# The second head's GpSimd operations in an attention and mixture-of-experts kernel, over all 128 partitions

## The chip, the cores and the metric

One core of a Trainium2 chip runs the whole kernel. The metric is the device time of one execution in microseconds (us). The kernel before takes 857.82 us, the median of three runs from 856.32 to 862.12 us. The rows below come from one profiled execution of it.

## The reference

The first part is causal attention over 8 batches of 8 heads, 576 tokens and 64 features each. To the scaled scores a bias from a running sum is added, and what lies behind the diagonal is masked. The second part sends every one of the 4608 rows of 512 to one of eight experts, the one with the largest gate logit.

```python
s_pos = np.maximum(s, 0.0)
cum = np.cumsum(s_pos, axis=-1)
bias = -(cum[:, :, :, None] - cum[:, :, None, :])
scores = np.where(causal, -1000000000.0, scores + np.minimum(bias, 0.0))
attn = np.exp(scores - np.max(scores, axis=-1, keepdims=True))   # then divided by its sum, times v
...
expert_idx = np.argmax(x @ w_gate, axis=1)
out[mask] = gate_w[mask, None] * (np.maximum(xe @ w1[e], 0.0) @ w2[e])
```

## The kernel before, in words

**Pairs.** Attention works on 32 pairs of heads, one pair after the other. Head 0 of a pair lies on partitions 0 to 63 and head 1 on 64 to 127. The 576 queries are cut into five groups. Groups 0 to 3 hold 128 queries of one head each. The last 64 queries of both heads make one *mixed* group (`MIX`): its q is laid out block-diagonally in a tile `qd`, head 0 in one quarter and head 1 in the other, with zeros elsewhere. There are two `qd` tiles, used in turn.

**Precision by halves.** q and k are each split into a high part and a low part (`q`, `kh`, `kl`). The scores of a group are three products: high by `kh`, high by `kl`, low by `kh`. In each pair TensorE (PE) begins with group 0, and its second product needs `kl`.

**The engines in a pair.** ScalarE (ACT) makes `kh`, the exponentials and some copies out of PSUM. VectorE (DVE) makes `z` (scores plus the mask table `B`, with the row's extreme) and other copies, among them `xb`, the attention output of a pair, once per pair. GpSimd (POOL) makes the high part of q (`QH`, line 198), `kl` (`KL`, line 210), the causal entries of the mask table (`DM`, lines 149 and 162 to 172), the low part of q (`QL`, line 203) and `qd` (`QD`, line 214), in this order. Before the change, `qd` is two copies, one for each head's 64 partitions, and the causal entries of the mixed group are two selects, again one for each head.

**Routing.** Four pairs are one batch. While the next four pairs run, the batch before is routed. Its 576 rows go to DRAM with five indirect DMAs per batch (*scatters*, line 465), which POOL issues: at `SD`, between the low part of q and `qd`, in two pairs of four, and at `SC`, between `kl` and the mask table, in three of four (the names are those of the table `ORDER`; all five are `xs<-xr,dsi` in the trace). The rows come from a tile `xr` with two buffers, so that a batch writes into the buffer that was used two batches earlier. `fresh` (line 351, an iota on POOL) is the first to write into it.

**Order.** The order of each engine's work inside the pair loop is written out by hand: `ORDER` lists one step per token, and all engines except SyncE (SP) keep that order. The framework adds a semaphore wait to an instruction wherever it sees a dependence. Waits on `DMASW` are for DMAs that POOL has issued, `DMAHW` for those of SP and ACT.

**After attention** the eight experts run one after the other, almost all of it matmuls on PE.

Of the kernel before, what the change touches and what calls it, by code (L numbers as in the profile page):

```python
# [8 lines left out]
F32 = mybir.dt.float32  # L9
# [4 lines left out]
AF = mybir.ActivationFunctionType  # L14
ALU = mybir.AluOpType
# [4 lines left out]
P, HP = 128, 64  # L20
# [33 lines left out]
UB, UW = 768, 1536  # L54
# [18 lines left out]
class Attention:  # L73
    def __init__(self, ctx, tc, K, qkv, s, rt, ps_t):
        self.tc, self.nc, self.K, self.qkv, self.rt, self.ps_t = tc, tc.nc, K, qkv, rt, ps_t
        nc = tc.nc
        pool = lambda name, bufs: ctx.enter_context(tc.tile_pool(name=name, bufs=bufs))
        self.open, self.st, self.nfill = True, {}, 0
        self.ldx, c0, self.lq, self.ld, self.ldv = (
            pool("a_x", 4), pool("a_c0", 1), pool("a_q", 2), pool("a_k", 2), pool("a_v", 4),  # L80
        )
        self.wk, c1, cp, self.sm = pool("a_wk", 4), pool("a_c1", 1), pool("a_c", 1), pool("a_sm", 10)
        self.qd = [c0.tile([P, 2, 2, HP], F32R, name=f"qd{i}") for i in range(2)]
        self.Es = [c1.tile([P, 2, w], F32, name=f"E{g}") for g, w in enumerate(TW[:4])]
        self.Es.append(c1.tile([P, 640], F32, name="E4"))
        self.aT = [(c0, cp)[i].tile([P, 5, 2, S], F32, name=f"aT{i}") for i in range(2)]
        self.ps_s = ctx.enter_context(tc.tile_pool(name="ps_s", bufs=2, space=PSUM))
        self.tab = pool("a_tab", 4)
        flat = self.aT[1].rearrange("p a h c -> p (a h c)")
        raw, cum, zz = (flat[:, S * x : S * x + S] for x in range(3))  # L90
        nc.vector.memset(zz, 0.0)
        for h in range(2):
            nc.sync.dma_start(raw[64 * h : 64 * h + 64], s)
        self.load(0)
        for i in range(2):
            nc.scalar.activation(
                self.qd[i].rearrange("p a h c -> p (a h c)"), zz[:, : 4 * HP], AF.Copy
            )
        self.eye = cp.tile([P, 3, HP], BF16, name="eye")
        self.tri = cp.tile([P, P], BF16, name="tri")  # L100
        low = self.Es[0][:, 0]
        nc.gpsimd.memset(low, 0.0)
        for h in range(2):
            self.keep_causal(low[64 * h : 64 * h + 64], low[64 * h : 64 * h + 64], [[-1, P]])
        nc.vector.tensor_scalar(out=raw, in0=raw, scalar1=0.0, scalar2=8.0, op0=ALU.max, op1=ALU.mult)
        nc.vector.tensor_tensor_scan(
            out=cum, data0=raw, data1=zz, initial=0.0, op0=ALU.add, op1=ALU.add
        )
        tc.keep_in_program_order(nc.scalar.dma_start(K["cum"], cum[:64]))
        self.load(1)  # L110
        self.load_v(0)
        self.cum = cum
        self.sel = cp.tile([P, 3, P], F32, name="sel")
        for x, h, c in (0, 0, slice(0, P)), (1, 65, slice(0, P)), (2, 0, slice(0, HP)), (2, 1, slice(HP, P)):
            one = K["ident"][:, h : h + 1]
            nc.vector.tensor_copy(self.sel[:, x, c], one.broadcast_to([P, c.stop - c.start]))
        b = self.st[0]["B"] = self.tab.tile([P, UW + S], F32, name="B")
        nc.gpsimd.memset(b, 0.0)
        for p in 1, 2:
            self.table(p)  # L120
        for part in (0, 2, 1, 3, 4):
            self.split(0, part)
        nc.vector.memset(self.eye, 0.0)
        nc.vector.tensor_tensor(
            out=self.eye[:, 1], in0=K["ident"][:, :HP], in1=K["ident"][:, HP:], op=ALU.add
        )
        nc.vector.tensor_copy(self.tri, low)

        warm = self.ps_s.tile([P, 2, 512], F32, name="s")[:, 0]
        zb = zz.bitcast(BF16)  # L130
        for _ in range(WARM):
            nc.tensor.matmul(warm, zb[:, :P], zb[:, P : P + 512], start=True, stop=True)
        for g in ORD[:2]:
            self.first_bias(g)
        nc.gpsimd.memset(self.Es[MIX][:, S:], 0.0)
        self.LT = rt.tile([P, 640], F32, name="LT", bufs=1)
        nc.gpsimd.memset(self.LT[:, S:], 0.0)
        self.xb, self.sums, self.sumx, self.rr, self.ra = [], [], [], [], []
        for i in range(2):
            self.xb.append(rt.tile([P, 4, 640], F32, name=f"xb{i}", bufs=1))  # L140
            nc.gpsimd.memset(self.xb[i][:, :, S:], 0.0)
            self.sums.append(rt.tile([P, 4, 8], F32, name=f"sums{i}", bufs=1))
            self.sumx.append(rt.tile([P, 4], F32, name=f"sumx{i}", bufs=1))
            self.rr.append(rt.tile([P, 5, 8], F32, name=f"rr{i}", bufs=1))
            nc.gpsimd.memset(self.rr[i][:, 4], 1.0)
            self.ra.append(rt.tile([P, 2, 5, 4], F32, name=f"ra{i}", bufs=1))
# [18 lines left out]
    def causal(self, p):  # L165
        t = self.st[p]["B"]
        b = t[:, :UW].rearrange("p (h k c) -> p h k c", h=2, c=P)
        self.keep_causal(b[:, :, 4:], b[:, :, :2], [[0, 2], [0, 2], [-1, P]])
        self.keep_causal(b[:, :, 3], b[:, :, 3], [[0, 2], [-1, P]])
        for h in range(2):  # L170
            x = t[64 * h : 64 * h + 64, UW + 512 :]
            self.keep_causal(x, x, [[-1, 64]])

    def load(self, p):
        x = self.ldx.tile([P, 2 * S], F32, name="qk")
# [15 lines left out]
    def split(self, p, part):  # L191
        nc = self.nc
        d = self.st[p]
        q, k = d["x"][:, :S], d["x"][:, S:]
        if part == 0:
            d["q"] = self.lq.tile([P, 2, S], F32R, name="q")
            if p > 1:
                nc.gpsimd.tensor_copy(d["q"][:, 0], q)
            else:
                nc.scalar.activation(d["q"][:, 0], q, AF.Copy)  # L200
        elif part == 1:
            e = nc.gpsimd if p > 1 else nc.vector
            e.tensor_tensor(out=d["q"][:, 1], in0=q, in1=d["q"][:, 0].bitcast(F32), op=ALU.subtract)
        elif part == 2:
            d["kh"] = self.ld.tile([P, S], F32R, name="kh")
            nc.scalar.activation(d["kh"], k, AF.Copy)
        elif part == 3:
            d["kl"] = self.ld.tile([P, S], F32R, name="kl")
            e = nc.gpsimd if p > 1 else nc.vector
            e.tensor_tensor(out=d["kl"], in0=k, in1=d["kh"].bitcast(F32), op=ALU.subtract)  # L210
        else:
            for h in range(2):
                r = slice(64 * h, 64 * h + 64)
                nc.gpsimd.tensor_copy(self.qd[p % 2][r, :, h], d["q"][r, :, 512:].bitcast(F32))

    def mms(self, groups, diagonal=None, begin=True):
        for n in range(len(groups[0][1])):
# [798 lines left out]
```

## Time and profile before

| | us |
|---|---|
| median of three runs | 857.82 |
| the profiled execution | 858.59 |
| its span, first to last instruction | 856.9 |
| PE busy in the span | 779.1 (91%) |
| DVE busy | 465.7 (54%) |
| ACT busy | 420.0 (49%) |
| POOL busy | 257.2 (30%) |
| mean granted clock of PE, as a share of full speed | 0.954 |

The 1.7 us between span and time are start and end of the execution. PE's clock has two levels here, 2.4 GHz (1.00) and 1.2 GHz (0.50), and a mean between them is a share of time at each. The pair loop fills about the first 393 us of the span, the experts the rest. `xb` copies mark the pairs on DVE, and some of them serve as borders of stretches below: they start at 71.97, 100.20, 138.07, 188.37, 237.57, 286.30 and 335.99 us, with three pairs in the first and in the second of these stretches and four in each later one.

### The profile page before, as it was taken

The page shows a single profiled execution, that of the slowest core. Times are in us where ns is not written, and L with a number is a line of the kernel's source. Part 1 is how long each engine was busy: PE and PEld are TensorE (multiplying, and loading weights), DVE is VectorE, ACT ScalarE, POOL GpSimd, SP SyncE. Part 2 cuts the span into 40 slices and gives each one's busy share as a digit, 9 for nine tenths or more (in the row PEclk, how much of TensorE's full clock was granted, in tenths as well). Part 3 has the DMA queues.
Part 4 walks back from the last instruction along what each step waited for, and adds up shares of the span by engine and source line. Part 5 has one row for each costly group of instructions (what it writes and reads, how often), then busy time and mean ns, then how long its engine had stood idle before and what let it go on. Part 6 is the DMA issues. An engine that isn't in the chain of part 4 may idle for free.

```text
span 856.9 us, 17576 instructions
## 1 busy us (share of the span) xinstructions
PE 779.1 (91%) x6664; PEld 603.3 (70%) x6664; DVE 465.7 (54%) x1234; ACT 420.0 (49%) x1003; POOL 257.2 (30%) x393
## 2 busy tenths in 40 slices
PE   7899979869796887888989999999999999999995
PEld 4667647656565666665778878788888888888874
DVE  4778858666685866766533536263264254442611
ACT  3788867757685676665313425151252242432510
POOL 4565556465455546632210010101001000001001
PEclk8999999988898998989999999999999999999998
DMA  7899745545554465144892626162062053440100
GB/s 246 241 285 305 201 140 183 186 146 155 185 188 134 162 194 157 54 161 149 265 280 79 212 74 222 64 222 87 26 205 105 26 176 125 158 165 28 54 28 37
DMA packets 57345, 130.80 MB, mean 153 GB/s; under 512 B 5456, under 2 KB 5456, under 8 KB 57233
## 3 DMA queue, kind: packets, MB, share of 16 engines
q1 hardware_dynamic: 48768, 105.53, 38.7%
q0 software_dynamic: 5936, 18.92, 5.9%
q10 hardware_dynamic: 2528, 4.89, 1.8%
q8 instruction: 67, 1.10, 0.5%
q14 instruction: 46, 0.37, 0.1%
HBM read 101.30 MB, written 28.27 MB: 151 GB/s over the span
## 4 chain that ended last, share of the span: by engine, by line
issue 36%; PE 11%; DMA 6%; another core or an unknown queue 3%; POOL 3%; DVE 2%; ACT 1%; POOLq 1%; DVEq 0%
DMA out_dram<-y,xr 6%; PE ph L723 3%; PE py L745 3%; POOL out_dram L752 2%; PE s L227 2%; PE t L336 2%; PE t L303 1%; DVE z L285 0%; DVE xr L456 0%; ACT aT L326 0%; PE s L303 0%; ACT E L299 0%; POOLq L845 0%; PE t L695 0%
## 5 line engine op out<-in xcount | busy, mean ns | idle before, releaser
L299 ACT ACTIVATE E<-z,m 128x128 f32<-128x128 f32 (+4 forms) x288 | 166.2, 581 | 96.8 <-DVE m L285 92.5
L745 PE MATMUL py<-w2t,hT 128*128 128x512 f32 x768 | 181.3, 392 | 1.0 <-DVEq L859 1.0
L723 PE MATMUL ph<-xT,w1t 128*128 128x512 f32 x768 | 177.7, 391 | 1.7 <-ACT xT L627 1.2
L723 PEld LDWEIGHTS ph<-xT,w1t 128*128 128x128 f32 x768 | 143.3, 188 | 33.0 <-issue 2.1
L745 PEld LDWEIGHTS py<-w2t,hT 128*128 128x128 f32 x768 | 142.6, 188 | 31.3 <-issue 1.4
L752 POOL DMA_INDIRECT out_dram<-y,xr x39 | 37.7, 966 | 397.4 <-DVE y L751 332.2
L285 DVE CUSTOM_DVE_ANT_0 z<-s,B 128x128 f32<-128x128 f32 (+3 forms) x224 | 114.0, 542 | 61.8 <-PE s L227 41.2
L227 PE MATMUL s<-kh,q 64*128 64x256 f32 (+3 forms) x512 | 102.9, 401 | 5.3 <-DVE m L285 4.0
L336 PE MATMUL t<-aT,v 128*64 128x64 f32 (+4 forms) x1152 | 97.4, 325 | 1.4 <-issue 0.7
L303 PE MATMUL t<-ident,E 64*128 64x64 f32 x1600 | 85.3, 237 | 5.5 <-issue 1.5
L751 DVE TENSOR_SCALAR y<-py,xr 128x512 f32<-128x512 f32 x35 | 26.3, 751 | 114.5 <-PE py L745 114.5
L725 ACT ACTIVATE hT<-ph 128x512 fp32r<-128x512 f32 x64 | 38.3, 598 | 102.2 <-PE ph L723 95.0
L303 PEld LDWEIGHTS t<-ident,E 64*128 64x128 f32 x1600 | 72.2, 148 | 17.9 <-issue 6.1
L227 PE MATMUL s<-kl,q 64*128 64x128 f32 (+3 forms) x256 | 46.6, 351 | 38.1 <-POOL kl L210 38.0
L726 DVE SCALAR_TENSOR_TENSOR hT<-ph,hT 128x512 fp32r<-128x512 f32 x64 | 44.1, 691 | 68.2 <-ACT hT L725 64.6
L227 PEld LDWEIGHTS s<-kh,q 64*128 64x128 f32 x512 | 55.6, 205 | 35.1 <-DVE m L285 14.6
L326 ACT COPY aT<-t 128x768 f32<-128x768 f32 (+2 forms) x96 | 73.2, 794 | 12.6 <-PE t L303 9.9
L336 PEld LDWEIGHTS t<-aT,v 128*64 128x64 f32 x1152 | 52.0, 142 | 23.5 <-issue 13.3
L149 POOL TENSOR_SCALAR_AFFINE_SELECT B<-B 64x64 f32<-64x64 f32 (+2 forms) x128 | 46.4, 385 | 50.3 <-issue 45.8
L227 PEld LDWEIGHTS s<-kl,q 64*128 64x128 f32 x256 | 27.8, 205 | 41.1 <-POOL kl L210 40.5
L299 ACT ACTIVATION_READ_ACCUMULATOR E<-z,m 128x1 f32 x288 | 54.9, 191 | 0.0
L465 POOL DMA_INDIRECT xs<-xr,dsi x40 | 40.1, 1002 | 34.3 <-issue 18.6
(156 smaller groups left out, 986.9 us busy)
## 6 DMA issues: line engine op xcount, KB each, us to landing
raw<-in_w_dram SPq DMA_DIRECT2D x32, 1024.0 KB, 5.6
qk<-in_qkv_dram SPq DMA_DIRECT2D x32, 576.0 KB, 4.1
B<-cum SPq DMA_DIRECT2D x31, 512.0 KB, 7.1
v<-in_qkv_dram SPq DMA_DIRECT2D x32, 320.0 KB, 6.0
B<-cum SPq DMA_DIRECT2D x62, 144.0 KB, 6.0
xr<-xs SPq DMA_DIRECT2D x8, 1028.0 KB, 5.2
xs<-blank ACTq DMA_DIRECT2D x9, 514.0 KB, 8.6
xs<-blank SPq DMA_DIRECT2D x8, 514.0 KB, 8.5
```

Source lines behind the costliest of these rows:

```text
L149: self.nc.gpsimd.affine_select(out=out, in_=src, pattern=pattern, compare_op=ALU.is_ge, fill=BIG, base=0, channel_multiplier=1,)
L227: self.nc.tensor.matmul(out, terms[n][0], terms[n][1], start=begin and n == 0, stop=n == len(terms) - 1, skip_group_check=True)
L285: ins = nc.vector.tensor_tensor_reduce(out=cut(z[:, :w]), in0=x, in1=mask, scale=-0.125, scalar=3.0e38, op0=ALU.add, op1=ALU.min, accum_out=m,
L299: nc.scalar.activation(out, z[:, :w], AF.Exp, bias=m, scale=-1.0, accum_out=total)
L303: self.nc.tensor.transpose(out, src[r], self.K["ident"][r, r])
L326: return self.nc.scalar.copy(o, i)
L336: nc.tensor.matmul(ps[64 * h : 64 * h + 64, bank, lo - 512 * bank : hi - 512 * bank], v[:, kt, h], self.aT[p % 2][:, kt, h, lo:hi], start= ...
L465: ins = self.nc.gpsimd.indirect_dma_start(out=self.K["xs"], out_offset=IndirectOffsetOnAxis(ap=r["dsi"][:n, k : k + 1], axis=0), in_=r["xr ...
L723: nc.tensor.matmul(ps, w[:, a, d, c], x[:, b, d], start=n == 0, stop=n == 11)
L726: nc.vector.scalar_tensor_tensor(out=h[:, 1, f], in0=ps, scalar=0.0, in1=h[:, 0, f].bitcast(F32), op0=ALU.max, op1=ALU.subtract)
L745: self.nc.tensor.matmul(ps, hT[:, a, f, c], w[:, b, f % 4], start=f == 0 and i == 0, stop=f == 7 and i == 2)
L752: disjoint(self.tc, "out", self.nc.gpsimd.indirect_dma_start(out=self.out, out_offset=IndirectOffsetOnAxis(ap=row[:, DM + 1 : DM + 2].bitc ...
```

## The change

`qd` is no longer two copies over 64 partitions each. Two selects over all 128 partitions write the halves of `qd`: one keeps partitions 0 to 63 and writes zeros on the rest, the other the reverse. With that, the zeros need not be written ahead, and two ACT instructions at the start of the program go. The mixed group's mask is no longer two selects of 64 by 64. A constant tile `mixed` (0 where allowed, -8e9 behind the diagonal) is copied once from `low`, and one addition over 128 partitions applies it.

```diff
--- before.py
+++ after.py
@@ -92,10 +92,6 @@
         for h in range(2):
             nc.sync.dma_start(raw[64 * h : 64 * h + 64], s)
         self.load(0)
-        for i in range(2):
-            nc.scalar.activation(
-                self.qd[i].rearrange("p a h c -> p (a h c)"), zz[:, : 4 * HP], AF.Copy
-            )
         self.eye = cp.tile([P, 3, HP], BF16, name="eye")
         self.tri = cp.tile([P, P], BF16, name="tri")
         low = self.Es[0][:, 0]
@@ -125,6 +121,8 @@
             out=self.eye[:, 1], in0=K["ident"][:, :HP], in1=K["ident"][:, HP:], op=ALU.add
         )
         nc.vector.tensor_copy(self.tri, low)
+        self.mixed = cp.tile([P, HP], F32, name="mixed")
+        nc.gpsimd.tensor_copy(self.mixed, low[:, :HP])
 
         warm = self.ps_s.tile([P, 2, 512], F32, name="s")[:, 0]
         zb = zz.bitcast(BF16)
@@ -167,9 +165,8 @@
         b = t[:, :UW].rearrange("p (h k c) -> p h k c", h=2, c=P)
         self.keep_causal(b[:, :, 4:], b[:, :, :2], [[0, 2], [0, 2], [-1, P]])
         self.keep_causal(b[:, :, 3], b[:, :, 3], [[0, 2], [-1, P]])
-        for h in range(2):
-            x = t[64 * h : 64 * h + 64, UW + 512 :]
-            self.keep_causal(x, x, [[-1, 64]])
+        x = t[:, UW + 512 :]
+        self.nc.gpsimd.tensor_tensor(out=x, in0=x, in1=self.mixed, op=ALU.add)
 
     def load(self, p):
         x = self.ldx.tile([P, 2 * S], F32, name="qk")
@@ -209,9 +206,11 @@
             e = nc.gpsimd if p > 1 else nc.vector
             e.tensor_tensor(out=d["kl"], in0=k, in1=d["kh"].bitcast(F32), op=ALU.subtract)
         else:
-            for h in range(2):
-                r = slice(64 * h, 64 * h + 64)
-                nc.gpsimd.tensor_copy(self.qd[p % 2][r, :, h], d["q"][r, :, 512:].bitcast(F32))
+            for base, h in (HP - 1, 0), (-HP, 1):
+                nc.gpsimd.affine_select(
+                    out=self.qd[p % 2][:, :, h], in_=d["q"][:, :, 512:].bitcast(F32), pattern=[[0, 2], [0, HP]],
+                    compare_op=ALU.is_ge, fill=0.0, base=base, channel_multiplier=2 * h - 1,
+                )
 
     def mms(self, groups, diagonal=None, begin=True):
         for n in range(len(groups[0][1])):
```

Per pair, POOL issues seven instructions apart from scatters where it issued eight. The orders of PE, ACT, DVE and SP are the same in both kernels from the second pair on, with their waits. At the start ACT loses the two instructions, and DVE puts the two low parts of pair 0 (q and `kl`) behind four small copies.

On POOL, in one of the pairs with a scatter at `SD`, around it (`q` in the first row is the low part, `CAST q` the high part of the next pair), the kernel before has:

```order
L203 TENSOR_TENSOR q<-qk,q 128x576 [waits Pool_49]
L465 DMA xs<-xr,dsi 38912x514
L214 CAST qd_101<-q 64x2x64 [waits Pool_49]
L214 CAST qd_101<-q 64x2x64 [waits DMASW3_49]
L198 CAST q<-qk 128x576 [waits DMAHW1_49,PE_49,Pool_49]
L210 TENSOR_TENSOR kl<-qk,kh 128x576 [waits Activation_49]
```

The changed kernel has there:

```order
L200 TENSOR_TENSOR q<-qk,q 128x576 [waits Pool_49]
L464 DMA xs<-xr,dsi 38912x514
L210 AFFINE_SELECT qd_101<-q 128x2x64 [waits Pool_49]
L210 AFFINE_SELECT qd_101<-q 128x2x64
L195 CAST q<-qk 128x576 [waits DMAHW1_49,PE_49]
L207 TENSOR_TENSOR kl<-qk,kh 128x576 [waits Activation_49]
```

The second of the two `qd` instructions lost its wait for the scatter, and the next one its wait for POOL.

A little further on POOL, from the scatter at `SC` to the iota of the next batch, the kernel before has:

```order
L465 DMA xs<-xr,dsi 38912x514 [waits DVE_49]
L149 AFFINE_SELECT B<-B 128x2x256 [waits DMAHW7_49]
L149 AFFINE_SELECT B<-B 128x2x128
L149 AFFINE_SELECT B<-B 64x64 [waits DMAHW0_49]
L149 AFFINE_SELECT B<-B 64x64 [waits DMAHW1_49,DMASW4_49,Pool_49]
L203 TENSOR_TENSOR q<-qk,q 128x576 [waits Pool_49]
L214 CAST qd_100<-q 64x2x64 [waits Pool_49]
L214 CAST qd_100<-q 64x2x64
L351 IOTA xr 128x5 [waits Pool_49]
L198 CAST q<-qk 128x576 [waits DMAHW6_49,PE_49]
```

The changed kernel has there:

```order
L464 DMA xs<-xr,dsi 38912x514 [waits DVE_49]
L147 AFFINE_SELECT B<-B 128x2x256 [waits DMAHW7_49]
L147 AFFINE_SELECT B<-B 128x2x128
L169 TENSOR_TENSOR B<-B,mixed 128x64 [waits DMAHW1_49,DMAHW0_49]
L200 TENSOR_TENSOR q<-qk,q 128x576 [waits Pool_49]
L210 AFFINE_SELECT qd_100<-q 128x2x64 [waits Pool_49]
L210 AFFINE_SELECT qd_100<-q 128x2x64
L350 IOTA xr 128x5 [waits DMASW3_49,DMASW2_49,DMASW4_49,DMASW1_49,DMASW0_49]
L195 CAST q<-qk 128x576 [waits DMAHW6_49,PE_49]
```

The select of 64 by 64 that waited for the scatter is gone, and its place is taken by an addition that waits for the two table DMAs alone. The iota now waits for five scatters. The one just ahead of it is among them.

## Rows read from the trace of the kernel before

**Rows 1.** Waits from 100.2 to 335.99: who waited for what: us, times, longest.

```profile
POOL qd L214 <- DMA xs<-xr,dsi: 52.5, 14, 5.8
POOL B L149 <- issue: 44.6, 10, 5.6
...
PE s L227 <- POOL kl L210: 38.0, 15, 5.9
```

**Rows 2.** Timeline of POOL (start, us, instruction, [idle before, releaser]), two scatters.

```profile
251.33 1.01 POOL L465 DMA_INDIRECT xs<-xr,dsi  x1 [0.15 <-issue]
252.34 0.30 POOL L214 CAST qd<-q 64x128 fp32r<-64x128 f32 x1
258.35 0.29 POOL L214 CAST qd<-q 64x128 fp32r<-64x128 f32 x1 [5.70 <-DMA xs<-xr,dsi]
...
260.89 1.00 POOL L465 DMA_INDIRECT xs<-xr,dsi  x1 [0.16 <-issue]
261.92 1.20 POOL L149 TENSOR_SCALAR_AFFINE_SELECT B<-B 128x512 f32<-128x512 f32 x3
267.64 0.24 POOL L149 TENSOR_SCALAR_AFFINE_SELECT B<-B 64x64 f32<-64x64 f32 x1 [4.53 <-issue]
```

**Rows 3.** Timeline of PE around the same scatters, where kl is awaited.

```profile
260.78 0.33 PE L227 MATMUL s<-kl,q 64*128 64x128 f32 x2 [2.43 <-POOL kl L210]
...
275.37 0.33 PE L227 MATMUL s<-kl,q 64*128 64x128 f32 x2 [4.00 <-POOL kl L210]
```

**Rows 4.** Stretches: length, busy us (count) PE PEld DVE ACT POOL, PEclk, DMA, GB/s.

```profile
71.97:100.20 28.23, 26.96 (x411) 19.76 (x411) 26.71 (x91) 24.80 (x68) 14.43 (x25) 1.00 0.82 241
100.20:138.07 37.87, 30.21 (x420) 22.05 (x422) 23.78 (x81) 24.64 (x68) 21.96 (x34) 0.91 0.51 164
138.07:188.37 50.30, 39.96 (x555) 29.25 (x555) 33.80 (x115) 33.18 (x91) 26.52 (x42) 0.93 0.52 163
188.37:237.57 49.20, 41.78 (x555) 30.69 (x555) 33.43 (x114) 33.44 (x91) 27.38 (x44) 0.86 0.54 167
237.57:286.30 48.73, 40.18 (x557) 29.07 (x555) 34.47 (x115) 33.33 (x91) 26.92 (x43) 0.93 0.53 169
286.30:335.99 49.69, 40.51 (x553) 29.99 (x555) 33.00 (x115) 33.24 (x91) 26.91 (x43) 0.90 0.52 165
...
500.00:600.00 100.00, 99.70 (x501) 81.06 (x498) 46.29 (x72) 33.87 (x62) 9.36 (x10) 1.00 0.41 141
```

**Rows 5.** Stretches around one long wait of PE: length, busy (count), PEclk, DMA, GB/s.

```profile
122.00:127.00 5.00, 0.00 (x0) 0.85 0.14 53
127.00:129.00 2.00, 1.88 (x30) 0.50 0.45 76
```

**Rows 6.** POOL's groups by shape: count, busy us, mean ns, idle before.

```profile
L214 POOL CAST qd<-q 64x128 fp32r<-64x128 f32 x64 | 19.3, 301 | 68.6 <-DMA xs<-xr,dsi 62.7 <-DVE q L203 4.3
L149 POOL TENSOR_SCALAR_AFFINE_SELECT B<-B 64x64 f32<-64x64 f32 x64 | 15.8, 246 | 47.3 <-issue 45.8 <-DMA B<-cum 0.2
L149 POOL TENSOR_SCALAR_AFFINE_SELECT B<-B 128x256 f32<-128x256 f32 x32 | 13.0, 407 | 0.0
L650 POOL TENSOR_TENSOR w1t<-raw,w1t 128x512 fp32r<-128x512 f32 x4 | 5.0, 1273 | 5.5 <-ACT w1t L649 5.5
...
L915 POOL TENSOR_SCALAR_AFFINE_SELECT low<-one 128x128 f32<-128x128 f32 x1 | 0.3, 294 | 0.1
```

**Rows 7.** Timeline of POOL in a pair without scatters: the high part of q.

```profile
86.83 0.67 POOL L198 CAST q<-qk 128x576 fp32r<-128x576 f32 x1 [3.57 <-PE s L227]
```

**Rows 8.** Timeline of POOL: the last scatter of a batch and its landing.

```profile
226.81 0.93 POOL L465 DMA_INDIRECT xs<-xr,dsi  x1 [0.16 <-issue]
...
232.72 0.24 POOL L149 TENSOR_SCALAR_AFFINE_SELECT B<-B 64x64 f32<-64x64 f32 x1 [3.77 <-issue]
```

**Rows 9.** Timeline of DVE and POOL at the program's start.

```profile
8.13 0.75 DVE L210 TENSOR_TENSOR kl<-qk,kh 128x576 fp32r<-128x576 f32 x1
8.28 1.12 POOL L214 CAST qd<-q 64x128 fp32r<-64x128 f32 x2 [4.27 <-DVE q L203]
```

**Rows 10.** The low part of q: count, ns min/median/max, first and last start.

```profile
L203 POOL TENSOR_TENSOR q<-qk,q x30: 1408/1418/1470, 25.4 to 358.4; 128x576 fp32r<-128x576 f32 x30
```

## The prediction, made before the changed kernel was run

> **What bounds the kernel now.** I read the waits first, then POOL's and PE's timelines, then a table by stretches.
>
> Between 100.2 and 335.99 us POOL stands idle twice as a habit: 52.5 us in 14 waits ahead of `qd`, until a scatter has landed, and 44.6 us in 10 waits ahead of a mask select, where the trace sees no releaser [rows 1]. The timeline shows the place: the scatter's issue ends, the head-0 `qd` copy runs at once, and the head-1 copy starts 5.70 us later; after the next scatter three selects run, and the head-1 select starts 4.53 us later [rows 2]. The order of instructions names the cause of both: those two instructions, and only those, carry a semaphore wait for the scatter just issued. The second kind, which the trace leaves at "issue", is thus the same wait.
>
> POOL is in order, so behind the late head-1 operation the high part of q and `kl` are late, and PE waits for `kl` in its second score product: 38.0 us in 15 waits in the same stretch [rows 1], 2.43 and 4.00 us of it behind the two scatters shown [rows 3]. This is on the path, since PE is nearly full otherwise: in the three pairs before the first late `kl` it is busy 26.96 of 28.23 us, with a clock of 1.00 [rows 4].
>
> A long wait also costs PE its clock. Over 122 to 127 us PE does nothing; in the next 2 us the granted clock is 0.50, the lower level of 1.2 GHz [rows 5]. The clock over the five stretches with late `kl` is 0.91, 0.93, 0.86, 0.93 and 0.90 [rows 4]. As twice the missing share times the length, this is 6.8 + 7.0 + 13.8 + 6.8 + 9.9 = 44.4 us at the lower level, 22.2 us of full-speed work lost at most, since part of that time is the wait itself.
>
> After attention PE is busy 99.70 of 100 us [rows 4], so what attention gains is kept to the end.
>
> **The change part by part.** *Instructions.* Per pair POOL loses two copies of 0.301 us and two selects of 0.246 us [rows 6]. It gains two selects of 128 by 128: 0.294 us in the row of that size; the bounds are this and the 0.407 us of 128 by 256 [rows 6], and I take the former since the size is the same. The addition of 128 by 64 I work out from two-input additions on POOL, 1.273 us at 512 columns [rows 6] and 1.418 at 576 [rows 10]: 2.27 ns a column, so 1.273 - 448 x 0.00227 = 0.26 us; the bounds are 0.1 and 0.41. Together 1.09 us go and 0.85 come: -0.25 us a pair, -8 us on POOL over 32 pairs. It is worth nothing by itself: where no scatter is issued, POOL waits 3.57 us for PE before it may write the next high part [rows 7]. That idle time is the cover; at the upper bounds POOL has 0.13 us more per pair, still inside it.
>
> *Waits removed.* The two scatter waits go from the head-1 operations: 52.5 + 44.6 = 97.1 us of POOL's idle time [rows 1]. With them the late `kl` goes, and the gain is what PE gets back. I size it in two ways. (a) The stretches from 100.20 to 335.99 hold 19 pairs in 37.87 + 50.30 + 49.20 + 48.73 + 49.69 = 235.8 us, 12.41 us a pair; the three pairs before them, routed too but with `kl` in time, take 28.23 / 3 = 9.41 [rows 4]. 19 x 9.41 = 178.8, so 57.0 us are to be had. (b) 38.0 us of waits and up to 22.2 us of clock give 38 to 60. Next in line at 9.41 us are DVE (26.71 of 28.23 busy) and ACT (24.80) [rows 4], so the pair can hardly fall below it. POOL has the room: 26.92 us of work in the four pairs from 237.57 [rows 4], less 1.0, against 4 x 9.41 = 37.6.
>
> *A wait added.* The iota waits for the five scatters of the batch that had its buffer last, and the youngest of them is the one issued just before. That scatter lands 232.72 - 227.74 = 4.98 us after its issue ended [rows 8]; between it and the iota now stand three mask instructions (1.20, as in rows 2), the low part of q (1.42) and two selects (0.59), 3.2 us. So the iota would wait 1.8 us, five times: 9 us on POOL. Behind it stand the high part of q and `kl`. The cover is POOL's 3.57 us [rows 7] less one scatter with its gap, 1.16 [rows 2], so 2.4 us, more than 1.8. Without that cover all 9 us would come back; I charge a quarter, 2 us.
>
> The Trainium skill puts a DMA issued by GpSimd at about 2.0 us plus its bytes over 436 GB/s ("DMA: Bandwidth & Descriptors", the section on the anatomy of one SWDGE DMA). For 128 rows of 2056 bytes this gives an estimate of 2.6 us, less than the 3.2 us in front of the iota, so no wait would be left and the gain would be 57. The trace disagrees with 4.98 us, and I go by the trace.
>
> *The start.* ACT loses two instructions while it waits for a load anyway. DVE's low parts of pair 0 move behind four small copies; I bound the effect by one such low part, 0.75 us [rows 9], either way, and take 0. The copy that makes `mixed` stands on POOL ahead of memsets that nobody awaits there; like the copies of `qd` it costs at most 0.3 us [rows 6]. No DMA is added or moved, and SP's queue keeps its order.
>
> *Sum.* 57 - 2 = 55 us. The profiled execution took 858.59, which becomes 803.6; the median shown is 0.8 us lower, so I say **803 us**.
>
> **The rivals.**
>
> *The wait moves, half comes back.* POOL's or DVE's next late piece keeps PE waiting for some `kl`, and the clock still falls. For it: POOL has two scatters in some pairs, landings may grow longer as the DMA share of 0.53 rises with the pace, and the iota's wait is new. Against it: POOL's idle time above. It gives back the 38 us of waits less the 9 us of the iota, up to the whole 38: 858.6 less 29 to 38 = 821 to 829, say 824.
>
> *Another chain is as long.* `kl` comes in time, but DVE and ACT, both near 90% busy in the fast pairs [rows 4], take over with scatters and higher pace together. A gain of a third, about 20 us: 838. Against it speaks that the same routing work ran at 9.41 us a pair at 0.82 of DMA [rows 4].
>
> *The change doesn't do what it says.* If POOL stood still because its own cores were busy with the scatter, an instruction over 128 partitions would stand still too, and the time stays at 858. Against it: the select of 128 by 512 begins 0.03 us after the issue ended (260.89 + 1.00 to 261.92) [rows 2].
>
> *Slower: POOL becomes the bound.* Packed against DVE, POOL's operations stretch. At the program's start two `qd` copies beside a DVE subtraction of two SBUF tensors took 1.12 us [rows 9] where two such take 0.60 [rows 6], 1.9 times. POOL would hold 25.9 us per four pairs; at 1.9 times this is 49 us, just the present length of a stretch, so from there on the kernel is slower. At 2.2 times, say, it would hold 57 us and lose 8 us in each of 4.75 stretches of four pairs (19 pairs): 897. Against it: inside the loop the low part of q takes 1.408 to 1.470 us in all 30 instances [rows 10], with DVE busy two thirds of the time, and DVE's frequent operations there read one operand from PSUM. The Trainium skill says that VectorE's second SBUF port is shared with GpSimd, so that GpSimd's instructions and VectorE's two-port ones block each other ("Advanced Engine Details and Errata", VectorE Performance Modes). The rows of the start agree; no row in the loop shows it.
>
> **How the numbers follow.** Forecast 0.65, half 0.22, another chain 0.06, no effect 0.04, slower 0.03. The forecast's own range is 797 to 812: the gain between 46 (all of the iota's 9 us paid, and 2 for other leftovers) and 60 (the upper end of b). To hold 8 in 10 the range takes in the half case as well: **796 to 829**. A measurement of this kernel tells about 1% from no change, 8.6 us. Faster by more than that are the first three cases, 0.93; within 1% the fourth, 0.04; slower the last, 0.03.
>
> **What would show it.** In the changed profile POOL's waits for `xs` ahead of `qd` and the idle time ahead of the mask operation should be gone, POOL should idle ahead of the high part of q instead, PE's wait for `kl` should fall from 38 us to under 5, PE's clock in these stretches should rise to 0.97 or more, and four pairs should take 38 to 40 us. The selects should show 0.29 us, the addition 0.26, the iota's wait 1 to 3 us. I am wrong if PE still waits for `kl`, now behind the iota (second case), if DVE's or ACT's waits grow by what `kl` lost (third), if POOL idles after a scatter without a semaphore to blame (fourth), or if POOL's low part of q takes well over 1.47 us (last).

## The result, and the profile of the changed kernel

The changed kernel takes 803.54 us (median of 4 runs, 802.27 to 806.24) against 859.39 us of the kernel before beside it (4 runs, 856.32 to 862.12). The ratio is 0.9355, with a 95% interval of 0.931 to 0.940. Its profiled execution took 802.42 us, 56.2 less than the profiled execution of before.

One correction to the text ahead of the prediction: two names are exchanged there. `SC` is the scatter between the low part of q and `qd`, in three pairs of four, and `SD` the one between `kl` and the mask table, in two of four. The prediction rests on the places in the rows, which carry their instructions, and not on the names.

First the waits of the kernel after, between the `xb` copies that start at 102.02 and 285.13 us. These are the same 19 pairs that began and ended at 100.20 and 335.99 before. The columns are us, times, longest.

```profile
POOL q L195 <- PE s L226: 43.3, 19, 3.3
...
PE s L226 <- DVE m L284: 5.1, 13, 0.5
...
POOL xr L350 <- DMA xs<-xr,dsi: 3.1, 4, 1.0
...
POOL xr L350 <- issue: 1.0, 1, 1.0
```

POOL waits for no scatter ahead of `qd` or the mask table any more, where it waited 97.1 us [rows 1]. PE's wait for `kl` is not among the answer's lines at all; it was 38.0 us [rows 1]. POOL now waits in each of the 19 pairs for PE, ahead of the high part of q, which tells that POOL is ahead. What is new is the iota's wait on line 350, five times, 4.1 us in all.

The stretches after (columns as in [rows 4]; three pairs in the first and the second, four in each later one):

```profile
73.14:102.02 28.88, 27.67 (x419) 20.80 (x419) 27.72 (x91) 24.27 (x66) 16.84 (x27) 1.00 0.84 253
102.02:131.73 29.71, 27.47 (x422) 20.18 (x422) 25.23 (x81) 25.00 (x69) 19.96 (x30) 1.00 0.71 210
131.73:170.09 38.36, 36.72 (x558) 26.96 (x557) 34.53 (x115) 33.15 (x91) 26.10 (x39) 1.00 0.73 214
170.09:208.59 38.50, 36.81 (x557) 27.06 (x557) 34.51 (x114) 33.23 (x91) 26.03 (x39) 1.00 0.73 214
208.59:246.86 38.27, 36.63 (x557) 26.97 (x557) 34.48 (x115) 33.15 (x91) 26.08 (x39) 1.00 0.73 215
246.86:285.13 38.27, 36.83 (x558) 26.99 (x557) 34.48 (x115) 33.14 (x91) 26.05 (x39) 1.00 0.69 207
```

Four pairs take 38.3 to 38.5 us where they took 48.7 to 50.3 [rows 4], the granted clock is 1.00 in every stretch, and PE is busy 95% of the 183.1 us that the last five rows hold (174.5 us). By these rows PE's own work is the bound now and no longer POOL's chain; no run changes PE's work in the kernel after, so this is read and not tested.

POOL's timeline around three scatters (start, us, instruction, idle before and its releaser):

```profile
180.44 1.01 POOL L464 DMA_INDIRECT xs<-xr,dsi  x1 [0.16 <-issue]
181.47 0.55 POOL L210 TENSOR_SCALAR_AFFINE_SELECT qd<-q 128x128 fp32r<-128x128 f32 x2
185.32 0.66 POOL L195 CAST q<-qk 128x576 fp32r<-128x576 f32 x1 [3.30 <-PE s L226]
185.95 1.42 POOL L207 TENSOR_TENSOR kl<-qk,kh 128x576 fp32r<-128x576 f32 x1
187.53 1.01 POOL L464 DMA_INDIRECT xs<-xr,dsi  x1 [0.16 <-issue]
188.56 1.00 POOL L147 TENSOR_SCALAR_AFFINE_SELECT B<-B 128x512 f32<-128x512 f32 x2
189.53 0.32 POOL L169 TENSOR_TENSOR B<-B,mixed 128x64 f32<-128x64 f32 x1
...
196.98 0.92 POOL L464 DMA_INDIRECT xs<-xr,dsi  x1 [0.17 <-DVE dd L409]
...
201.96 0.14 POOL L350 IOTA xr<- 128x5 int32 x1 [0.77 <-DMA xs<-xr,dsi]
204.26 0.67 POOL L195 CAST q<-qk 128x576 fp32r<-128x576 f32 x1 [2.17 <-PE s L226]
```

Both selects run right behind the issue, and so does the addition behind its two selects, where the kernel before stood idle 5.70 and 4.53 us [rows 2]. The iota waits 0.77 us, and POOL still waits 2.17 us for PE after it: the added wait lies in idle time.

POOL's groups by shape, which answer to [rows 6]:

```profile
L195 POOL CAST q<-qk 128x576 fp32r<-128x576 f32 x30 | 19.9, 665 | 85.5 <-PE s L226 85.5
L210 POOL TENSOR_SCALAR_AFFINE_SELECT qd<-q 128x128 fp32r<-128x128 f32 x64 | 18.1, 307 | 7.4 <-DVE q L200 6.2
L169 POOL TENSOR_TENSOR B<-B,mixed 128x64 f32<-128x64 f32 x32 | 10.8, 336 | 0.3 <-DMA B<-cum 0.3
...
L350 POOL IOTA xr<- 128x5 int32 x8 | 1.1, 142 | 4.1 <-DMA xs<-xr,dsi 3.1 <-issue 1.0
```

The selects take 0.307 us, the addition 0.336. Idle time ahead of `qd` is down from 68.6 us to 7.4, and ahead of the mixed part of `B` from 47.3 to 0.3.

### The profile page after: what moved, and what is told of

Same layout as the page of the kernel before. It is cut to its first block, busy times and chain, and to the rows that moved or that the text cites. A ratio compares the mean times of both kernels' runs of the same rounds, so it can differ in the third digit from the quotient of the medians.

```text
span 800.7 us, 17488 instructions
## 1 busy us (share of the span) xinstructions
PE 758.1 (95%) x6664; PEld 587.1 (73%) x6664; DVE 471.4 (59%) x1234; ACT 417.6 (52%) x1001; POOL 250.1 (31%) x362
## 4 chain that ended last, share of the span: by engine, by line
issue 39%; PE 27%; DVE 16%; DMA 7%; another core or an unknown queue 4%; POOL 3%; ACT 2%; POOLq 1%; DVEq 0%; ACTq 0%
PE s L226 9%; DMA out_dram<-y,xr 6%; DVE z L284 5%; PE t L302 5%; PE t L335 5%; PE ph L722 3%; PE py L744 3%; POOL out_dram L751 2%; DVE xb L324 2%; DVE xr L455 2%; ACT aT L325 1%; DVE dd L409 1%; DVE aT L324 1%; DVE sm L422 1%
## 5 line engine op out<-in xcount | busy, mean ns | idle before, releaser
L298 ACT ACTIVATE E<-z,m 128x128 f32<-128x128 f32 (+4 forms) x288 | 166.0, 581 | 47.3 <-DVE m L284 44.9
L226 PE MATMUL s<-kh,q 64*128 64x256 f32 (+3 forms) x512 | 95.6, 376 | 9.4 <-DVE m L284 7.6
L302 PE MATMUL t<-ident,E 64*128 64x64 f32 x1600 | 80.6, 227 | 5.7 <-ACT kh L203 1.3
L302 PEld LDWEIGHTS t<-ident,E 64*128 64x128 f32 x1600 | 68.2, 139 | 19.0 <-issue 8.4
L226 PEld LDWEIGHTS s<-kh,q 64*128 64x128 f32 x512 | 51.1, 189 | 38.6 <-DVE m L284 25.1
L464 POOL DMA_INDIRECT xs<-xr,dsi x40 | 40.0, 1000 | 38.3 <-issue 17.9
L626 ACT ACTIVATE xT<-t 128x512 fp32r<-128x512 f32 x32 | 17.6, 597 | 61.9 <-PE t L694 58.9
L195 POOL CAST q<-qk 128x576 fp32r<-128x576 f32 x30 | 19.9, 665 | 85.5 <-PE s L226 85.5
L627 DVE TENSOR_TENSOR w2t<-raw,w2t 128x512 fp32r<-128x512 f32 x64 | 41.2, 684 | 5.6 <-ACT w2t L626 5.6
```

The costliest lines, as they stand in the source:

```text
L226: self.nc.tensor.matmul(out, terms[n][0], terms[n][1], start=begin and n == 0, stop=n == len(terms) - 1, skip_group_check=True)
L298: nc.scalar.activation(out, z[:, :w], AF.Exp, bias=m, scale=-1.0, accum_out=total)
L302: self.nc.tensor.transpose(out, src[r], self.K["ident"][r, r])
L464: ins = self.nc.gpsimd.indirect_dma_start(out=self.K["xs"], out_offset=IndirectOffsetOnAxis(ap=r["dsi"][:n, k : k + 1], axis=0), in_=r["xr ...
L627: b = self.nc.vector.tensor_tensor(out=lo, in0=src, in1=hi.bitcast(F32), op=ALU.subtract)
```

## The experiments

The theory: in pairs with scatters POOL's in-order chain (its work and the waits for a scatter's landing) set the pace, and PE's waits for `kl` and its lower clock followed from it. The rivals: POOL's own cores are busy with the scatter; PE's fallen clock is a loss of its own; the cheaper instructions bring the gain. Ratios are to the kernel before, run beside each one. "Loop" is the time from the first to the last `xb` copy.

| kernel | us | ratio (95%) | POOL waits for scatters | PE waits for kl | loop |
|---|---|---|---|---|---|
| before | 857 to 860 | 1 | 108.5 | 38.0 | 357.3 |
| after | 803.5 | 0.9355 (0.931 to 0.940) | 4.1 | 0 | 299.0 |
| 1: waits put back | 854.5 | 0.9943 (0.9918 to 0.9969) | 113.0 | 38.7 | 351.4 |
| 2: `qd` alone | 825.3 | 0.9626 (0.9571 to 0.9682) | 46.0 | 6.4 | 320.9 |
| 3: mask alone | 841.2 | 0.9816 (0.9764 to 0.9868) | 90.1 | 29.4 | 337.8 |
| 4: PE kept busy, scores changed | 873.2 | 1.0181 (1.0123 to 1.0238) | - | - | - |
| 5: PE kept busy | 860.2 | 1.0018 (0.9986 to 1.0049) | 106.2 | 24.5 | 357.5 |
| 6: after, selects twice | 803.7 | 0.9353 (0.9301 to 0.9406) | 1.5 | 0 | 303.3 |
| 7: before, more POOL work | 873.0 | 1.0156 (1.0094 to 1.0217) | 109.1 | 51.1 | 372.9 |
| 8: before, head 1 first | 868.8 | 1.0104 (1.0035 to 1.0172) | 118.0 | 36.9 | 370.9 |
| 9: before, scatters later | 834.0 | 0.9736 (0.9668 to 0.9805) | 41.9 | 10.1 | 331.8 |

The waits are sums over the whole span of POOL's idle time ahead of `qd`, the mask table and (in the kernel after and in 6) the iota; 108.5 is 62.7 + 45.8, of which 97.1 lie in the 19 pairs of [rows 1]. In row 2 the trace puts 16.6 of the 46.0 us down to the mask table's load. These are four waits of the head-1 select, each until 4.7 to 6.3 us after a scatter's issue ended, and that load is awaited for 0.6 us in the kernel after; so I count them as the scatter's.

**1. The waits put back.** The changed kernel, with a dependence on the scatter just issued added to the second select and to the addition.

```diff
+        self.landed(self.nc.gpsimd.tensor_tensor(out=x, in0=x, in1=self.mixed, op=ALU.add))
...
+    def landed(self, ins):
+        if self.last:
+            after(self.tc, ins, [self.last])
+        self.last = None
...
+            self.landed(ins)          # the second select of qd
...
+        self.last = disjoint(self.tc, "xs", ins).name   # behind each scatter
```

> The changed kernel, with the two waits for the scatter just issued put back by hand: on the second select of qd and on the addition of the mask. All other instructions are those of the changed kernel. Theory (the waits alone cost the time): back to the kernel before, 854 to 862 us, PE waits about 38 us for kl, its clock falls to about 0.9 in the stretches with scatters. Rival (the instructions over 128 partitions are the gain, being cheaper or fewer): it stays at about 803 us. In between, say 830: both share.

It took 854.49 us (852.3 to 856.92), as expected. Its waits (us, times, longest) in 100 to 340 us:

```profile
POOL qd L215 <- DMA xs<-xr,dsi: 58.4, 15, 6.2
POOL B L169 <- DMA xs<-xr,dsi: 46.1, 10, 5.8
...
PE s L232 <- POOL kl L212: 38.7, 15, 5.2
```

All of [rows 1] is back, `kl`'s wait included, and the clock over its 19 pairs is 0.92 (stretch row, with the same columns as above):

```profile
104.64:337.40 232.76, 190.47 (x2636) 139.87 (x2638) 157.09 (x532) 157.54 (x427) 125.42 (x183) 0.92 0.53 168
```

So the waits carry the loss, 51 of the 56 us. All else that the change does is worth 4.9 us here (859.38 - 854.49; 2.7 to 7.0 by the interval). This is also the case against POOL's cores being busy: the same select over 128 partitions runs at once after a scatter in the kernel after, and 4.54 us later here (third row; the select in the second carries no wait):

```profile
196.28 1.03 POOL L470 DMA_INDIRECT xs<-xr,dsi  x1 [0.78 <-DVE base L451]
197.32 0.30 POOL L215 TENSOR_SCALAR_AFFINE_SELECT qd<-q 128x128 fp32r<-128x128 f32 x1
202.17 0.29 POOL L215 TENSOR_SCALAR_AFFINE_SELECT qd<-q 128x128 fp32r<-128x128 f32 x1 [4.54 <-DMA xs<-xr,dsi]
```

**2 and 3. One part each.** The first keeps the two selects per head for the mask and changes `qd` alone; the second keeps the two `qd` copies (and the zeros written at the start) and changes the mask alone. Each is the change's own diff less the other's lines.

> Only qd is written over 128 partitions; the mixed group's mask is again two selects of 64 partitions, and the second of them waits for both kinds of scatters. Theory (a wait counts as far as it exceeds POOL's idle time ahead of the high part of q, 1.8 to 3.3 us in the changed profile): the mask's waits of 4 to 5 us are late by 1 to 2.6 us in two pairs of four, so 812 to 825 us, likeliest 815. Rival (each wait keeps POOL as late as both did): 850 or more. Rival (only the wait ahead of qd counts, since kl stands right behind it): 803.

> Only the mask is one addition over 128 partitions; qd is again two copies of 64 partitions, the second of which waits. Theory (excess over POOL's idle time): waits of 4.5 to 5.7 us in three pairs of four, late by 1.5 to 3 us each, so 820 to 835 us, likeliest 828, with PE waits for kl of 12 to 25 us. Rival (both waits are needed for POOL to be late): 803 to 808. Rival (each keeps POOL late): 850 or more.

`qd` alone gave 825.25 us (821.24 to 828.19), at the edge of its expectation and 10 us over the likeliest value. PE's waits for `kl` alone do not make the rest: between 103.02 and 303.65 us, the same 19 pairs, PE waits 6.2 us for `kl` and 9.0 us for DVE's `m` (5.1 in the kernel after), and it is busy 6.8 us longer, at a clock of 0.97. The mask alone gave 841.19 us (837.27 to 845.18), above the 820 to 835 expected and below the 850 of the rival. In the waits of the second (whole span) the reason is seen:

```profile
POOL qd L215 <- DMA xs<-xr,dsi: 90.1, 23, 6.3
PE s L228 <- POOL kl L211: 29.4, 15, 3.7
```

The mask's 45.8 us are gone, but those ahead of `qd` rise from 62.7 to 90.1: the head-1 copy, the next one of its kind, takes over a part of the wait for the scatter that the mask select no longer waits for. Net 18.4 us of waits go, and the loop is 19.5 us shorter. The two gains, 34 and 18 us, add up to 52, the change's own is 56.

**4 and 5. The clock by itself.** The kernel before, with 56 matmuls of 128 columns put between the first and the second product of group 0, where PE used to wait for `kl`, in five pairs (11, 15, 19, 23, 27); their results are read by nobody.

```diff
+            if n == 1 and spin is not None:
+                for _ in range(SPIN):
+                    self.nc.tensor.matmul(spin, self.tri, self.tri, start=True, stop=True, ...)
...
+        spin = ps[:, 1, 256:384] if g == 0 and 11 <= p <= 27 and p % 4 == 3 else None
```

> The kernel before, with all its waits, and 56 idle matmuls of 128 columns (results unused) on PE in the pairs where kl is awaited longest (pairs 11, 15, 19, 23 and 27), between the first and the second product of group 0, where PE otherwise stands idle for 4 to 6 us. They take some 3.5 us at full clock. Theory (the fallen clock after such a wait is a cost of its own, up to 3 us each time): PE's clock stays up, and the kernel is 8 to 15 us faster than before, 844 to 851 us. Rival (other engines hide the low clock): no change, 858. Rival (the idle matmuls overrun the wait): up to 10 us slower.

It took 873.16 us (870.17 to 876.49), far outside the expectation, and it answers another question than the one I asked. The attention ended at 391.60 us, as before (392.95). The time was lost in the experts, which depend on the data through the routing:

```profile
391.60:869.80 478.20, 459.66 (x2317) 373.25 (x2317) 198.84 (x331) 151.27 (x281) 46.78 (x48) 0.99 0.36 123
```

The kernel before has 2269 PE instructions and 463.90 us there. So the routing had changed, and with it, as far as one can tell from that, the scores, though the dummy matmuls with `start=True, stop=True` write other columns. The same kernel with `start=False, stop=False` has 2269 again:

> As the spin before, with idle matmuls that do not clear what the first product has written in the same bank, so that scores and routing stay those of the kernel before. Theory, new (POOL's chain sets the pace there, so PE's clock costs nothing by itself): attention ends when it did, 855 to 863 us, though PE spends 10 us or more less at the lower clock. Old theory (the fallen clock is a cost of its own): 844 to 851 us.

This one took 860.19 us (855.63 to 863.49, 10 runs), no change. Its stretches, at the times of [rows 4] and [rows 5]:

```profile
100.20:138.07 37.87, 33.70 (x495) 24.39 (x490) 25.69 (x85) 26.09 (x72) 21.89 (x35) 1.00 0.52 164
138.07:188.37 50.30, 43.30 (x609) 32.48 (x609) 33.70 (x112) 33.12 (x91) 27.16 (x43) 0.93 0.53 164
188.37:237.57 49.20, 42.49 (x611) 31.66 (x611) 34.90 (x116) 33.59 (x93) 26.66 (x43) 0.97 0.51 167
237.57:286.30 48.73, 41.88 (x601) 32.17 (x603) 31.69 (x106) 32.46 (x89) 24.86 (x39) 0.93 0.53 169
286.30:335.99 49.69, 43.19 (x621) 31.88 (x617) 35.39 (x118) 33.27 (x90) 27.52 (x46) 0.97 0.50 165
...
122.00:127.00 5.00, 4.50 (x68) 3.44 (x63) 1.60 (x4) 1.68 (x6) 3.06 (x6) 1.00 0.14 53
127.00:129.00 2.00, 0.78 (x20) 0.78 (x22) 0.16 (x1) 0.00 (x0) 1.84 (x2) 1.00 0.00 0
```

PE is busy 4.50 of the 5.00 us in which it did nothing before, and the clock of the five longer stretches is 1.00, 0.93, 0.97, 0.93 and 0.97 where it was 0.91, 0.93, 0.86, 0.93 and 0.90: 19.8 us at the lower level, worked out as in the prediction, against 44.4. PE's wait for `kl` fell from 38.0 to 24.5 us, and the loop is as long as before, 357.5 us. Behind the dummy matmuls PE still waits for `kl` in all five pairs, 0.46 to 3.56 us, so they did not overrun the wait either. A higher clock and less waiting on PE bought nothing, since `kl` came no sooner. In the kernel before, the fallen clock is thus a consequence of the waits and no loss beside them, as far as the 24.6 us that were given back can show.

**6 and 7. POOL's work by itself.** The changed kernel with its two `qd` selects issued twice, and the kernel before with its head-1 `qd` copy issued three times (some 0.6 us more POOL work per pair in either).

```diff
-            for base, h in (HP - 1, 0), (-HP, 1):
+            for base, h in ((HP - 1, 0), (-HP, 1)) * 2:
...
-            for h in range(2):
+            for h in (0, 1, 1, 1):
```

> The changed kernel, with each of the two selects of qd issued twice: 0.55 us more of POOL per pair, 18 us over all pairs. Theory (POOL has idle time in every pair now, 1.7 us or more ahead of the high part of q): no change, 801 to 808 us, and the idle time ahead of the high part of q shrinks by about 0.55 us a pair. Rival (POOL still sets the pace): up to 18 us slower, 821 us.

> The kernel before, with the head-1 copy of qd issued three times: some 0.7 us more of POOL per pair, all of it behind the wait for the scatter. Theory (in the pairs with scatters POOL's chain of work and landings sets the pace): the 19 pairs with scatters take 0.6 to 0.7 us more each, 870 to 874 us against 859. Rival (PE's own work at the fallen clock sets the pace, and POOL is late only now and then): 859 to 863 us.

The first took 803.68 us (801.61 to 806.17), the same as the changed kernel. In the profiled executions its span is 1.7 us longer and its loop 4.4 us, and POOL's idle time ahead of the high part of q shrank from 85.5 to 75.6 us, 0.33 us a pair where 0.55 were expected. The second took 873.03 us (870.75 to 876.29), 15.7 more than before (8 to 19 by the interval), and its loop is 15.6 us longer. Its waits in the whole span:

```profile
POOL qd L214 <- DMA xs<-xr,dsi: 61.7, 18, 6.0
PE s L227 <- POOL kl L210: 51.1, 19, 6.8
POOL B L149 <- issue: 47.4, 11, 5.6
```

The waits for scatters are as before; PE waits 13.1 us longer for `kl`. Two more copies of 0.297 us in the 24 pairs from 100.20 us on are 14.3 us. So POOL's work counts in full in the kernel before. In the kernel after it hardly counts: its selects are busy 16 us longer (34.0 against 18.1), and the medians show none of that, though the interval leaves room for 4 to 5 us.

**8. Which instruction waits.** The kernel before, with head 1 ahead of head 0 in `qd` and in the mask.

```diff
-        for h in range(2):
+        for h in (1, 0):
```

> The kernel before, with head 1 ahead of head 0 in both places. In the built order the wait for the scatter stays with head 1, so it now stands on the first of the two instructions. Theory (the framework's wait goes with the instruction that begins at partition 64, wherever it stands): POOL waits as long, and head 0's instruction of 0.25 to 0.3 us comes behind the landing instead of ahead of it: 859 to 866 us. Rival (the wait goes with the second instruction, or with POOL's cores that serve the upper partitions and are free by themselves): 803 to 850 us.

It took 868.8 us (865.68 to 872.91), a little over the 859 to 866 expected. The rival, that the second instruction waits whichever it is, falls: POOL's timeline shows head 1 waiting and head 0 behind it, both in one row, where a copy ran ahead of the wait before [rows 2].

```profile
259.86 1.00 POOL L465 DMA_INDIRECT xs<-xr,dsi  x1
265.70 0.63 POOL L214 CAST qd<-q 64x128 fp32r<-64x128 f32 x2 [4.83 <-DMA xs<-xr,dsi]
```

So head 0's operation no longer runs while the scatter lands but after it, 0.30 us in 18 pairs and 0.25 in 11: 8.2 us, where 3 to 15 were measured by the interval.

**9. More work between the scatter and head 1.** The kernel before, its instructions unchanged, but the scatter ahead of `qd` moved behind `qd`, and the one ahead of the mask selects moved behind them, by two entries of the table `ORDER`.

```diff
-... R30:0 SD:1 ca:0 X10:0 R31:0 X30:0 rv1:1 DM:-2
+... R30:0 ca:0 X10:0 R31:0 X30:0 rv1:1 DM:-2 SD:1
...
-... E2:0 E4:0 SC:-1
+... E2:0 E4:0
...
-S4:-1 KH:-2 R21:-1 R20:-1 T3:0 X21:-1 QD:-2 R40:-1 ...
+S4:-1 KH:-2 R21:-1 R20:-1 T3:0 X21:-1 QD:-2 SC:-1 R40:-1 ...
```

> The kernel before, with each scatter moved later on GpSimd so that more work stands between it and the next head-1 operation: the one that stood between the low part of q and qd comes behind qd (high part of q 0.67, kl 1.42 and three selects 1.20 us stand between), the one that stood ahead of the mask selects comes behind them (the low part of q 1.42 and one copy 0.30 us). Theory (the head-1 instruction waits for the landing, some 5.7 to 6.0 us after the issue's end, and POOL's chain sets the pace): of each wait goes what stands between: 14 waits of up to 5.7 us become about 2.7, 10 of up to 4.5 become about 4.0, so of 97 us about 20 to 45 go; PE's waits for kl fall from 38 to 10 to 25 us, and the kernel takes 820 to 845, likeliest 832. Rival (what costs is the scatter's issue or landing wherever it stands): 850 to 862. Second rival (any distance lets kl be in time): 803 to 812.

It took 834.0 us (831.9 to 834.17), where the theory had 832. POOL's timeline shows both places:

```profile
181.96 1.03 POOL L465 DMA_INDIRECT xs<-xr,dsi  x1 [1.77 <-DVE aT L325]
186.26 0.66 POOL L198 CAST q<-qk 128x576 fp32r<-128x576 f32 x1 [3.27 <-PE s L227]
186.90 1.40 POOL L210 TENSOR_TENSOR kl<-qk,kh 128x576 fp32r<-128x576 f32 x1
188.26 1.48 POOL L149 TENSOR_SCALAR_AFFINE_SELECT B<-B 128x512 f32<-128x512 f32 x4
...
199.78 1.00 POOL L465 DMA_INDIRECT xs<-xr,dsi  x1 [0.31 <-POOL B L149]
200.85 1.41 POOL L203 TENSOR_TENSOR q<-qk,q 128x576 fp32r<-128x576 f32 x1
202.33 0.28 POOL L214 CAST qd<-q 64x128 fp32r<-64x128 f32 x1
207.53 0.29 POOL L214 CAST qd<-q 64x128 fp32r<-64x128 f32 x1 [4.92 <-DMA xs<-xr,dsi]
```

Behind `qd` the scatter lands while POOL waits for PE and makes the high part and `kl`, and no mask select waits for it any more. Behind the masks too little work follows, and `qd` still waits 41.9 us in 11 waits. The time hit the expectation, the waits did not: of the 97.1 us in the 19 pairs 56.0 went (41.1 are left), where 20 to 45 were expected. The move has a price that the expectation left out. DVE's `sc` (line 414), a step of the routing, now waits 7.8 us in three waits for a scatter, and 6.4 us in two that the trace leaves at "issue" (before: 0.6 us in one), and PE waits 20.8 us for DVE's `m`, against 5.4 before and 10.1 for `kl` here. So that 834 came so near to 832 is in part luck. This move brings not quite half of the gain (some 25 of 56 us; 17 to 29 by the interval) without a new instruction; whether another placement brings more was not tried.

## Why the prediction was right, step by step

803 us was forecast, 803.5 came. The mechanism was right; some terms were off and made up for each other, so that the number is this near is luck.

- **POOL waits for scatters just issued, and two instructions carry the wait.** Right, and shown in both directions by experiments 1, 2 and 3. That an idle time whose releaser the trace calls "issue" is the same wait came from the order of instructions; experiment 1, where the trace names the scatter for it, bears it out (46.1 us in 10 waits, against 44.6 in 10 [rows 1]).
- **The gain of 57 us in the 19 pairs.** It was 235.8 - 183.1 = 52.7, at 9.64 us a pair and not 9.41. The three pairs that I took for a model were too short a sample: the same three pairs of the kernel after take 28.88 us, with 419 PE instructions between their borders against 411 in the row of before [rows 4]. Nor do they hold "the same routing work", as the second rival has it: in the kernel before only one scatter falls into them, at 93.50 us, where four later pairs hold five. The next five pairs gave 5.4 us more (57.0 from 335.99 to 392.95 before, 51.6 from 285.13 to 336.73 after), which the sum had left out. The first pair ends 2.2 us later. 52.7 + 5.4 - 2.2 and 0.3 in the first seven pairs make the 56.2 us; from the last `xb` copy to the end both kernels take 464 us.
- **The gain sized the other way, waits and clock.** As a count it holds: PE lost 38.0 us of waits and is busy 18.2 us less for the same pairs (192.6 in [rows 4], 174.5 after). As a cause the second term fails: experiment 5 gave PE more than half of its clock back, and no time. The lower end, 38, which would have held with the clock gone for good, was no bound on its own.
- **Costs of the instructions.** The selects took 0.307 us against 0.294. The addition took 0.336 against 0.26, inside its bounds; a line through two long additions does not reach down to 64 columns. POOL's total fell by 7.1 us against 8. "Worth nothing by itself" holds, within a few us, for the kernel after (experiment 6), where the idle time ahead of the high part of q covers it. In the regime before it fails: there a microsecond of POOL costs a microsecond (experiment 7), and experiment 1 was 4.9 us faster than before with all its waits. I had read the cover from a pair without scatters [rows 7], where it exists; in pairs with scatters there was none.
- **The iota's wait.** 4.1 us in five waits where I had 9; it waited 0.77 us in the timeline above, where the scatter had landed 4.06 us or less after its issue ended (201.96 - 197.90), sooner than the 4.98 of [rows 8]. It is hidden, as argued, and the 2 us that I charged were not paid. One row was a thin base for 4.98: in the kernel before, the 29 waits for a scatter ended between 2.0 and 6.8 us after the issue. That scatter is the last of its batch and has 64 rows (576 less four times 128), not the 128 of the prediction. By the Trainium skill's fit ("DMA: Bandwidth & Descriptors", the section on the anatomy of one SWDGE DMA) 64 rows give an estimate of 2.3 us (128 rows: 2.6), and no wait would be left; the trace shows one, a small one.
- **The start.** I took 0 and bounded it by 0.75 us; both were too low. The first pair ends at 37.77 us, 2.2 us later. ACT's timeline shows what the two lost instructions had carried (before, then after):

```profile
0.82 1.28 ACT L96 ACT_TABLE_LOAD   x1 [0.82 <-PEq L1002]
6.74 0.68 ACT L200 ACTIVATE q<-qk 128x576 fp32r<-128x576 f32 x1 [3.91 <-DMA qk<-in_qkv_dram]
...
6.81 0.52 ACTq L105 DMA_DIRECT2D cum<-aT  x1
7.37 1.28 ACT L197 ACT_TABLE_LOAD   x1 [7.37 <-DVE sel L112]
8.66 0.68 ACT L197 ACTIVATE q<-qk 128x576 fp32r<-128x576 f32 x1
```

The load of ACT's function table, 1.28 us, stands ahead of ACT's first activation. With the zeros written first it ran while ACT had to wait for the data; without them it delays the first copy of q. In experiment 2, which issues the `cum` DMA at 6.18 us (6.17 before), that copy starts at 8.03 instead of 6.74. So it is in all four kernels with the new start (after, experiments 1, 2 and 6: load at 6.74 to 7.37 us, first `xb` copy at 37.2 to 39.2), while the seven with the old start load the table at 0.8 us and have that copy at 33.8 to 37.8. The two means lie 2 us apart. Some 1.3 to 2 us of the gain are lost there; no run put the early load back to measure it alone.
- **The rivals.** None came. The low part of q takes 1.415 us on POOL, the same as before [rows 10], so nothing stretched. DVE's `m` now holds PE back 5.1 us in 19 pairs, too little for the chain that I had feared.

What stays open is why the framework puts the wait on the instruction that begins at partition 64. Experiment 8 shows that it goes with head 1, and the kernel after that instructions over all partitions do not get it; neither shows the rule.

## What to carry to other kernels

Ask of each wait on an in-order engine whether the data needs it. Here an instruction waited for a DMA that touches none of its tiles, and another form of the same instruction did not. Look for the engine whose work and waits together fill the time: before, POOL's 129.7 us of work [rows 4] and 97.1 of waits [rows 1] made 96% of the 235.8 us, while its busy share alone looked harmless at 30%; a busy neighbour with a fallen clock can be a symptom. And before an instruction goes as useless, look in the trace for what comes with it: here the zeros went, and a table load moved onto the path. Two cheap probes tell cause from symptom: a little more work on each suspect, and see which one makes the kernel longer.

## What the runs showed of the hardware

- POOL's waits for a scatter end 2.0 to 6.8 us after its issue ended in the kernel before (29 waits, nine of them at 2.0 to 2.5, the others from 4.05 on: 6.01 in [rows 2], 4.98 in [rows 8]); in experiment 9 one row above has 6.75 (207.53 - 200.78), in the kernel after the iota's waits end at 3.96 to 4.29.
- A GpSimd select over 128 partitions that also writes zeros costs 0.307 us, the copy of half as many partitions 0.301 [rows 6]. The two are different instructions, but twice the partitions cost next to nothing here.
- A matmul with its start and stop flags set into unused columns changed what came of other products (experiment 4: 2317 PE instructions in the experts against 2269, none with both flags off). The Trainium skill says that a matmul with the flag of a first one clears the written marks of the whole 2 KiB bank in the quadrants of 32 partitions that it writes, so that a later product there overwrites and does not add ("PSUM — Partial Sum Buffer", The four PSUM rules). That fits; no run here separates it from other causes.
- The load of ACT's function table took 1.28 us and came with the first activation in every kernel here: at 0.8 us where that one writes zeros, at 6.74 to 7.37 us where it copies q.
- PE's granted clock stayed at 1.00 from 122 to 129 us when matmuls filled its idle time (experiment 5); without them it was 0.50 from 127 to 129 us [rows 5].
